# A linear-attention and gated long-convolution kernel: head pairs with packed tails, crossbar transposes, a maximum added by matmul, a DFT split by parity, and a planned order

## The chip, the cores and the metric

One core of one Trainium2 chip. The metric is the device time of one execution in microseconds (us), the median of several; executions fall into a fast and a slow state, and only fast ones are compared. Engines: PE (TensorE), DVE (VectorE), ACT (ScalarE), POOL (GpSimd), SP (SyncE, which here only issues transfers). DMA is the set of 16 transfer engines; the profile counts every queue's packets against them.

## The reference, cut to what matters

```python
# q, k, v: 8 batches x 8 heads x 576 x 64; w_phi 64 x 128
def phi(x):
    proj = einsum('bhsd,df->bhsf', x, w_phi)
    proj = proj - max(abs(proj), axis=-1, keepdims=True)
    return concatenate([exp(proj), exp(-proj)], axis=-1)
q_p, k_p = phi(q), phi(k)
kv = einsum('bhsf,bhsd->bhfd', k_p, v);  z = sum(k_p, axis=2)
attn = (q_p @ kv) / (q_p @ z + 1e-06)           # -> x: 8 x 576 x 512
x1, x2, x3 = split(x @ w_proj, 3)               # w_proj 512 x 1536
x2_conv = irfft(rfft(x2, axis=1) * rfft(filter_fft, axis=0), axis=1)
out = (x1 * x2_conv * x3) @ w_out               # w_out 512 x 512
```

Two halves: attention per batch and head, then a gating block per batch. The maximum over 128 features makes rows of q and k comparable; the convolution is done as a DFT by matmul.

## The kernel before

Heads go in pairs. For a pair, q and k are transposed on PE against an identity and evicted by ACT. The 576 rows are five chunks of 128 (the last half empty), each handled by instructions of its own. The code is shortened; lines are left out inside and between the functions.

```python
def load_stage(nc, pools, q, k, v, b):
    for (src, dst) in ((q, qs), (k, ks), (v, vs)):
        for (ci, s0, rows) in s_chunks():                 # 15 loads a batch, rows of 64
            nc.gpsimd.dma_start(out=dst[0:rows, ci, :, 0:HDIM],
                in_=src[b, :, s0:s0 + rows, :].rearrange("h p d -> p h d"))

def tr_group(nc, pools, cdict, stage_t, hp, zero_pad, name):
    for (ci, s0, rows) in s_chunks():
        nc.tensor.transpose(trp[:, ci, :], blk, ident)
    nc.scalar.copy(dst, trp.rearrange("p c x -> p (c x)"))

# pk_group: wpp is block-diagonal, so both heads of a pair use all 128 rows
        nc.tensor.matmul(dst, lhsT=kT[:, s0:s0 + PART], rhs=wpp, start=True, stop=True)
# pqn_group: the maximum of q only scales one of the two signs afterwards
    nc.scalar.activation(cq, mxq, AF.Exp, bias=0.0, scale=2.0)
# nem_group, nep_group: one pass a sign, joined on DVE
    nc.vector.tensor_tensor(out=tmp, in0=full_view, in1=cq_b, op=ALU.mult)
    nc.vector.tensor_tensor(out=NEt, in0=full_view, in1=tmp, op=ALU.add)
    nc.vector.tensor_tensor(out=out_view, in0=num_view, in1=r_b, op=ALU.mult)
# xt_group: the attention's result is transposed on PE as well
        nc.tensor.transpose(trp[:, ci, :], x_nat[:, ci, t * PART:(t + 1) * PART], ident)
# g_fwd: six groups of five matmuls a batch (3 cosine, 3 sine)
            for kt in range(5):
                nc.tensor.matmul(acc, lhsT=mat[:, kt, m * PART:(m + 1) * PART],
                                 rhs=x2n[:, kt, :], start=(kt == 0), stop=(kt == 4))
```

The gating block of batch b is interleaved with the attention of batch b+1. A round below is one such pair.

## Time and profile before

| | before |
|---|---|
| time, median of 3 (range) | 506.72 us (505.07 to 511.94) |
| busy PE / DVE / ACT / POOL | 402.8 / 357.6 / 307.3 / 200.3 us |
| transfers issued by POOL (q0) | 114432 packets, 47.4% of the DMA engines' time |
| head, until the first gating matmul | 73.4 us |
| seven rounds | 56.7 us each; 50.9 in the last two |
| tail, the last gating block alone | 35 us |

Busy is the union of an engine's instructions, matmul ends being modelled. A round that waits for nothing is the busiest engine's work plus its gaps; the head is a chain, where latencies add up. The lines that carry this are in the prediction.

### The profile page before, as it was taken

To read this page: it belongs to the slowest core of one execution; us is meant where nothing else is said; L and a number is where in the kernel's file an instruction comes from. 1 tells how busy PE (TensorE), PEld (TensorE's weight loads), DVE (VectorE), ACT (ScalarE), POOL (GpSimd) and SP (SyncE) were. 2 spreads that over 40 slices of the span, in tenths; PEclk is the share of its full clock that TensorE was granted. 3 is DMA by queue.
4 is the path that set the end of the run, shared out by engine and by line. 5 is a ranking of instruction groups with operands and counts; after the bars stand their busy time and mean duration, and the time that the engine had idled before them with its cause. 6 is when DMAs were issued, how large, how long until landed. Compare 5 with 4: busy or idle time off the path is not lost.

```text
span 505.9 us, 9253 instructions
## 1 busy us (share of the span) xinstructions
PE 402.8 (80%) x3672; PEld 240.8 (48%) x3734; DVE 357.6 (71%) x546; ACT 307.3 (61%) x611; POOL 200.3 (40%) x212
## 2 busy tenths in 40 slices
PE   1566559988688796879798795888888898889995
PEld 0344435555355553545455463554545554555442
DVE  2267654497567884697859785697777986798664
ACT  1669858877079633985189352994279636963220
POOL 9789921158012860346312760246512211221000
PEclk9856659999899998998999798998999999999999
DMA  9999970059610893039900796019910011001102
GB/s 84 176 144 95 95 47 1 0 33 78 75 54 1 53 94 89 2 21 75 124 19 1 50 75 113 1 11 74 99 53 2 2 43 53 0 2 43 53 1 95
DMA packets 119724, 26.92 MB, mean 53 GB/s; under 512 B 113472, under 2 KB 114560, under 8 KB 119680
## 3 DMA queue, kind: packets, MB, share of 16 engines
q0 software_dynamic: 114432, 16.88, 47.4%
q1 hardware_dynamic: 5248, 9.44, 5.4%
q8 instruction: 29, 0.48, 0.4%
q14 instruction: 15, 0.12, 0.1%
HBM read 33.75 MB, written 9.44 MB: 85 GB/s over the span
## 4 chain that ended last, share of the span: by engine, by line
PE 48%; DVE 20%; ACT 15%; DMA 6%; POOL 6%; issue 5%; DVEq 0%; POOLq 0%; ACTq 0%
PE acc L598 7%; PE acc L656 7%; PE acc L568 6%; DVE x_nat L404 5%; PE acc L613 5%; DMA out_dram<-o 4%; ACT Epk L274 3%; PE acc L689 3%; ACT Emk L276 3%; PE trp L256 3%; DVE mxk L278 2%; PE xtr L411 2%; PE acc L540 2%; PE KV L355 2%; DVE NEt L397 2%
## 5 line engine op out<-in xcount | busy, mean ns | idle before, releaser
L414 ACT COPY xT<-xtr 128x640 bf16<-128x640 bf16 x32 | 22.5, 702 | 78.6 <-PE xtr L411 78.6
L278 DVE TENSOR_REDUCE mxk<-Pk_m 128x8 f32<-128x1024 f32 x32 | 39.1, 1221 | 41.8 <-ACT Emk L276 41.7
L337 DVE TENSOR_REDUCE mxq<-Pqn_m 128x8 f32<-128x1024 f32 x32 | 39.0, 1218 | 14.7 <-PE Pqn_m L335 14.4
L411 PE MATMUL xtr<-ident,x_nat 128*128 128x128 bf16 x160 | 16.3, 240 | 39.9 <-DVE x_nat L404 39.9
L598 PE MATMUL acc<-wproj_sb,xT 128*128 128x512 bf16 x153 | 44.3, 411 | 3.6 <-ACT qT L258 3.3
L240 POOL DMA_DIRECT2D qs<-in_q_dram x40 | 34.5, 874 | 27.4 <-PE trp L256 20.1
L274 ACT ACTIVATE Epk<-Pk_m 128x1024 bf16<-128x1024 f32 x32 | 32.7, 1022 | 19.2 <-PE Pk_m L272 19.2
L689 PE MATMUL acc<-wout_sb,yT 128*128 128x512 bf16 x146 | 39.8, 388 | 3.4 <-DVE yT L661 2.5
L602 DVE CAST x2n<-acc 128x512 bf16<-128x512 f32 (+1 forms) x40 | 26.9, 687 | 20.2 <-PE acc L598 20.1
L694 DVE COPY o<-acc 128x512 f32<-128x512 f32 (+1 forms) x40 | 27.2, 679 | 18.9 <-DMA out_dram<-o 9.4
L240 POOL DMA_DIRECT2D ks<-in_k_dram x40 | 33.9, 878 | 10.1 <-PE trp L256 10.1
L404 DVE TENSOR_TENSOR x_nat<-NEt,r 128x640 bf16<-128x640 f32 x32 | 35.6, 1111 | 0.6
L319 ACT ACTIVATE Eq<-Pq_m 128x1024 bf16<-128x1024 f32 x32 | 34.1, 1065 | 2.9 <-PE Pq_m L313 2.9
L568 PE MATMUL acc<-xT,wproj_sb 128*128 128x512 bf16 x120 | 35.3, 421 | 0.4
L240 POOL DMA_DIRECT2D vs<-in_v_dram x40 | 34.1, 881 | 2.8 <-POOL v_518 L296 0.6
L321 ACT ACTIVATE Eqm<-Pq_m 128x1024 bf16<-128x1024 f32 x32 | 33.8, 1058 | 0.0
L411 PEld LDWEIGHTS <-x_nat 128*128 128x128 bf16 x160 | 10.9, 106 | 48.0 <-DVE x_nat L404 46.1
L540 PE MATMUL acc<-xT,wproj_sb 128*128 128x512 bf16 x121 | 31.4, 378 | 2.7 <-ACT x1s L544 2.4
L613 PE MATMUL acc<-x2n,fwdS 128*128 128x512 bf16 x117 | 29.1, 378 | 5.3 <-ACT Cxs L617 5.0
L276 ACT ACTIVATE Emk<-Pk_m 128x1024 bf16<-128x1024 f32 x32 | 33.1, 1033 | 0.0
L661 DVE TENSOR_TENSOR yT<-acc,ts 128x512 bf16<-128x512 f32 x32 | 22.0, 688 | 12.8 <-PE acc L656 7.8
L572 DVE TENSOR_TENSOR ts<-acc,x1s 128x512 bf16<-128x512 f32 x32 | 22.0, 690 | 12.1 <-PE acc L568 10.0
(315 smaller groups left out, 1066.0 us busy)
## 6 DMA issues: line engine op xcount, KB each, us to landing
out_dram<-o SPq DMA_DIRECT2D x32, 256.0 KB, 2.0
qs<-in_q_dram POOLq DMA_DIRECT2D x32, 128.0 KB, 4.1
ks<-in_k_dram POOLq DMA_DIRECT2D x32, 128.0 KB, 4.5
vs<-in_v_dram POOLq DMA_DIRECT2D x32, 128.0 KB, 4.8
wproj_sb<-in_moe_w_proj_dram POOLq DMA_DIRECT2D x4, 384.0 KB, 8.3
out_dram<-o SPq DMA_DIRECT2D x8, 128.0 KB, 2.2
qs<-in_q_dram POOLq DMA_DIRECT2D x8, 64.0 KB, 3.9
ks<-in_k_dram POOLq DMA_DIRECT2D x8, 64.0 KB, 4.2
```

The costliest lines, as they stand in the source:

```text
L240: nc.gpsimd.dma_start(out=dst[0:rows, ci, :, 0:HDIM], in_=src[b, :, s0:s0 + rows, :].rearrange("h p d -> p h d"))
L274: nc.scalar.activation(Epk[:, 0:4, :], Pk_m, AF.Exp, bias=0.0, scale=1.0)
L276: nc.scalar.activation(Emk[:, 0:4, :], Pk_m, AF.Exp, bias=0.0, scale=-1.0)
L278: nc.vector.tensor_reduce(out=mxk[:, 0:4, :], in_=Pk_m.rearrange("p c (h f) -> p c h f", h=2), axis=AX.X, op=ALU.max, apply_absolute_value ...
L337: nc.vector.tensor_reduce(out=mxq[:, 0:4, :], in_=Pqn_m.rearrange("p c (h f) -> p c h f", h=2), axis=AX.X, op=ALU.max, apply_absolute_valu ...
L404: nc.vector.tensor_tensor(out=out_view, in0=num_view, in1=r_b, op=ALU.mult)
L411: nc.tensor.transpose(trp[:, ci, :], x_nat[:, ci, t * PART:(t + 1) * PART], ident)
L540: nc.tensor.matmul(acc, lhsT=wproj[:, kt, m * PART:(m + 1) * PART], rhs=xT_sb[:, kt, 0:512], start=(kt == 0), stop=(kt == 3))
L568: nc.tensor.matmul(acc, lhsT=wproj[:, kt, 1024 + m * PART:1024 + (m + 1) * PART], rhs=xT_sb[:, kt, 0:512], start=(kt == 0), stop=(kt == 3))
L598: nc.tensor.matmul(acc, lhsT=xT_sb[:, kt, s0:s0 + PART], rhs=wproj[:, kt, 512:1024], start=(kt == 0), stop=(kt == 3))
L613: nc.tensor.matmul(acc, lhsT=mat[:, kt, m * PART:(m + 1) * PART], rhs=x2n[:, kt, :], start=(kt == 0), stop=(kt == 4))
L689: nc.tensor.matmul(acc, lhsT=yT[:, kt, s0:s0 + PART], rhs=wout[:, kt, :], start=(kt == 0), stop=(kt == 3))
```

## The change

The intent is to take work off PE and DVE: transposes of q, k and the attention's result go to the DMA crossbar; the two heads of a pair sit in the two 64-row halves of PE; the tails of 64 rows of different heads are packed; q's maximum is added inside PSUM by a matmul, so that both signs accumulate in one numerator; the DFT is split into even and odd frequencies over folded inputs (17 matmuls for 30); and one list, PLAN, fixes the order on every engine. The core of the diff, shortened, with lines left out inside the functions too:

```diff
-        for (ci, s0, rows) in s_chunks():
-            nc.gpsimd.dma_start(out=dst[0:rows, ci, :, 0:HDIM], ...)
+    def load(self, n, b):                       # one load of rows of 256 elements
+        main = src[:, 0:512, :].rearrange("h (p j) d -> p h (j d)", j=4)
+        self.nc.gpsimd.dma_start(out=self.at(n + "n", b)..., in_=main)
-        nc.tensor.transpose(trp[:, ci, :], blk, ident)
-    nc.scalar.copy(dst, trp.rearrange("p c x -> p (c x)"))
+    def tr(self, n, b, i=None):
+            self.nc.sync.dma_start_transpose(out=self.at(n + "T", b), in_=self.at(n + "n", b))
...
+    def nat(self, n, b, hp):
+        for w_ in range(2):
+            for jj in range(2):
+                for jp in range(2):
+                    a = (2 * w_ + jj) * 128
+                    r = slice(64 * jp, 64 * jp + 64)
+                    self.mm(self.pb(jp, a, a + 128), x[r, (2 * hp + w_) * 2 + jj, :], w[r, :],
+                            True, True)
+    def Pq(self, b, hp):                        # q transposed, minus its maximum
+        for jp in range(2):
+            self.mm(self.pb(jp), w[r, :], x[r, 4 * hp:4 * hp + 4, :], start=True, stop=False)
+        for w_ in range(2):
+            for jp in range(2):
+                self.mm(self.pb(jp, 256 * w_, 256 * w_ + 256), sel[r, 2 * hp + w_, :],
+                        mT[r, jp:jp + 3:2, :], start=False, stop=(w_ == 1))
-    nc.vector.tensor_tensor(out=NEt, in0=full_view, in1=tmp, op=ALU.add)
+    def NE(self, b, hp):                        # both signs in one PSUM group
+                for s, g in enumerate("pm"):
+                    self.mm(self.pb(w, 65 * j, 65 * j + 65), ..., KVs[:, hp, w, s, :],
+                            start=(s == 0), stop=(s == 1))
+    def trx(self, b, hp):
+        self.nc.sync.dma_start_transpose(out=self.at("xT", b)[:, hp, :]..., in_=self.at("xn", b)...)
+    def fold(self, b, odd):                     # even and odd parts, on POOL
+        self.nc.gpsimd.tensor_tensor(out=o, in0=x[:, :, :, 0:56], in1=x[:, :, :, 72:128], op=op)
...
+        for word in PLAN.split():
+            name, _, bank = word.partition("@")
+            getattr(self, f)(*[int(a) if a.isdigit() else a for a in args])
```

The start of PLAN (a word is an operation, a batch, a part and a PSUM bank):

```
load,k,0 gen_phase filt_load gen_rows zeros gen_half load,q,0 gen_cols@0 w_load,phi load,v,0
gen_cols_ev@0 gen_angles loadt,k,0 tr,k,0 loadt,v,0 loadt,q,0 tr,q,0 w_load,proj gen_sin Pk,0,1@2
... w_load,out ... load,v,1 load,k,1 ... load,q,1 ... Qn,0,0@4 ... mlo,0 trm,0 ... tr,k,1
```

## The prediction

> **What bounds the kernel now.** I read, in this order: the busy line and the slices of the page; the core split into head, steady stretch and tail; the waits and the chain; the timeline of the tensor engine, for the pace of each kind of matmul; last the DMA queues.
>
> ```profile
> PE 402.8 (80%) x3672; PEld 240.8 (48%) x3734; DVE 357.6 (71%) x546; ACT 307.3 (61%) x611; POOL 200.3 (40%) x212
> ...
> q0 software_dynamic: 114432, 16.88, 47.4%
> ```
>
> PE is the busiest engine and DVE is not far below; one queue, the POOL-issued loads, holds the DMA engines for half the span.
>
> ```profile
> 0.00:73.40 73.40, 37.62 (x290) 25.18 (x293) 38.74 (x80) 46.90 (x88) 59.04 (x81) 0.70 1.36 110
> 312.00:363.00 51.00, 45.52 (x434) 27.54 (x438) 39.17 (x56) 34.36 (x70) 23.67 (x23) 0.93 0.52 36
> 420.00:470.00 50.00, 44.45 (x444) 26.93 (x449) 40.94 (x59) 34.88 (x71) 11.54 (x8) 1.00 0.06 20
> 470.00:506.00 36.00, 29.29 (x184) 14.08 (x187) 19.44 (x28) 6.82 (x12) 0.00 (x0) 0.97 0.13 45
> ```
>
> Columns: window, length, busy us of PE, PEld, DVE, ACT, POOL, clock, DMA share, GB/s. The first gating-block matmul (L598) starts at 73.4 us; until then only batch 0's attention and the set-up run. Seven rounds follow, each batch b's gating block beside batch b+1's attention: 73.4 to 470.7, 397 us, 56.7 a round. The last gating block runs alone for 35 us. In the chain of waits the rounds are 56 to 60 us long while loads run (chain entries "DMA vs" 5.2 us, "DMA out_dram" 5.9 and 6.3 us) and 50.9 once they have ended (x2 starts at 369.3, 420.2, 470.7 us). There PE is busy 89% and DVE 82%: the steady round is PE-bound, with DVE close behind.
>
> ```profile
> 231.31 0.44 PE L256 MATMUL trp<-ident,ks 128*128 128x128 bf16 x5
> 231.59 1.89 PE L568 MATMUL acc<-xT,wproj_sb 128*128 128x512 bf16 x7
> 233.31 0.60 PE L272 MATMUL Pk_m<-wpp,kT 128*128 128x256 bf16 x4
> 233.75 0.27 PE L272 MATMUL Pk_t<-wpp,kT 128*128 128x256 bf16 x1
> ...
> 234.16 0.63 PE L584 MATMUL acct<-xT,wproj_sb 128*128 128x64 bf16 x16
> 234.63 0.32 PE L355 MATMUL KV<-v_2722,Epk 128*128 128x65 bf16 x5
> 234.79 0.32 PE L355 MATMUL KV<-v_2724,Emk 128*128 128x65 bf16 x5
> ```
>
> The mean ns of a group is latency; the pace is start to start. 5 transposes in 0.28 us are 56 ns each; 4 of 256 columns in 0.44 are 110; 16 of 64 columns in 0.47 are 29; 5 of 65 in 0.16 are 32; 512 columns take 215 (8 matmuls, one unrecorded, in 1.72). Per batch, now: 60 transposes 3.4 us; k and q projections 40x110 = 4.4; transposed q 8x215+8x54 = 2.2; KV, NEm, NEp 160x32 = 5.1; x1 and x3 32x215+32x29 = 7.8; x2 4.3; forward DFT 30x215 = 6.4; inverse 24x215+24x29 = 5.9; output 4.3. Sum 43.8, against a 50.9 us round: PE at 86% of its own pace.
>
> ```profile
> 327.94 0.95 DVE L624 TENSOR_TENSOR t_4195<-Cxs,HC 128x1536 bf16<-128x1536 bf16 x1
> 328.80 2.03 DVE L626 TENSOR_TENSOR t_4197<-Cxs,HS 128x1536 bf16<-128x1536 bf16 x1
> ```
>
> ```profile
> 328.56 1.46 POOL L292 TENSOR_TENSOR v_4161<-vs,em 128x650 bf16<-128x650 bf16 x1 [5.12 <-ACT em L285]
> 329.98 1.99 POOL L296 TENSOR_TENSOR v_4163<-vs,mxe 128x650 bf16<-128x650 bf16 x1
> ```
>
> These are the timelines of DVE and of POOL in one stretch. The same DVE product takes 0.95 us alone and 2.03 beside POOL; the POOL product takes 1.28 alone (most of its groups) and 1.99 beside DVE.
>
> **What the Trainium skill says.** (1) "TensorEngine Tiling (Array Packing)", Overview and Tiling Modes: with a contraction of at most 64 rows the array runs as two 64-row tiles, up to 2x, but changing the tiling mode drains the engine. Every matmul of the attention here is 128*128, so this trace shows neither. (2) "SBUF — State Buffer", Who interferes with whom: DVE (two SBUF inputs) and GpSimd hold a shared port pair as an exclusive lock. The trace agrees: DVE's 2.03 us end at 330.83, 0.8 us after POOL's product has ended at 330.02, and POOL's next one runs 1.1 us past that. (3) "DMA: Bandwidth & Descriptors", Specifications: 512 B is the smallest efficient piece. 113472 of 119724 packets here are under it. (4) "VectorE: DVE Perf Modes", The three transpose paths: a crossbar transpose of 128x128 takes 1309 ns, one on TensorE 390. No transposing DMA is in this trace; PE's cost 219 ns of latency, 56 of pace, plus an eviction of 0.7 us for five.
>
> **The change, part by part (per batch).**
> *PE.* The 60 transposes go (-3.4 us). Natural k and q projections become 72 matmuls of 64 rows by 128 columns, 72x55 = 4.0 us one after another, 2.0 if the two row halves run together. Transposed q with the q maximum added by matmul: 8x215 + 18x110 + 4x55 = 3.9, or 2.0. KV stays 80x32 = 2.6. The numerator needs one pass (the exponent already holds the maximum; both signs accumulate in PSUM): 64x32 + 8x56 = 2.5. x1, x3 7.8, x2 4.3 and output 4.3 stay. The parity split takes the forward DFT from 30 to 17 matmuls (3.7) and the inverse from 24+24 to 20+20 (4.9). Sum 30.1 + 4.0 = 34.1 paired, 38.0 not. About 15 groups use half the rows; entering and leaving each may drain the array. The exposed part of a matmul's latency is 219-56 = 0.16 us, so at most 30x0.16 = 4.8; I take 2. PE: 36 (40 unpaired) against 43.8.
> *ACT.* 12 transpose evictions go (12x0.7 = 8.4), and 16 tail exponentials of about 0.4 become 2 of 1024 columns. Left: 18 exponentials at 0.95 start to start = 17.1; 7 tiny ones 1.5; from the plan 107 of 152 evictions of 512 columns in eight batches, 13.4x0.63 = 8.4, and KV's 0.8. Sum 28, against 35 now.
> *DVE.* 8 maxima of 1024 at 1.15 = 9.2 and two of 512, 1.2; reciprocals 1.0; normalising straight out of PSUM 4x0.69 + 2x0.41 = 3.6; spectral products five, 4x0.68 + 0.42 = 3.1, plus about 3 of lock waits (POOL is in use some 60% of the time, one product 1 to 2 us); ts and yT products 6.3; evictions 45/8 x 0.66 + KV's and tails' 1.2 = 4.9. Sum 32, against 42. tmp, NEt (3.3 each) and half the spectral products are what goes.
> *POOL.* v scaling: 4x(1024/650x1.28 = 2.0) and two tails 2.7; folds 3.5+1.4; t2 products 4x1.0; three loads at 0.87, six small at 0.6. Sum 26: no bound.
> *DMA.* Main loads move 1 KB rows in place of 256 B: 24576+12288 packets in place of 114432. Crossbar transposes add 1.9 MB a batch through the SP queue in ten issues; an estimate from the skill's 1309 ns for 32 KB taken as latency, not pace, is that they fit. They put 2 to 4 us of latency after each head pair, which the order hides in the steady state and not in the head.
>
> **The sum.** Steady round: 36 us of PE at 88%, the share it now reaches in the undisturbed windows (the planned order and fewer packets should keep it there all through, not only at the end) = 41. Seven rounds: 287. Head: the plan issues the first gating matmul after batch 0's attention; ACT needs by then about 31 us (18+4 exponentials, sines, filter evictions), DVE 29 after the first k projection. k lands at about 7 us (q's first megabyte takes from 1.3 to 10.4 now, in four times the packets), its transpose at about 13, a guess; then q maxima, the maximum's transpose, exponentials, normalising and the last transposes chain to 48-50. I take 52 (now 73.4). Tail: PE 7.8+4.3+3.7+4.9+4.3 = 25, plus fold, last eviction and store about 7 = 32 (now 35). 52+287+32 = 371; I add 3 for queue accidents: 374.
>
> **Rivals.** (a) The halves don't run together and mode changes drain fully: PE 38+5 = 43, /0.88 = 49 a round, 52+343+32 = 427. Against it: the code alternates row halves and banks on purpose. (b) DVE or its lock with POOL becomes the bound: POOL grows from 20 to 26 us a batch, so 32 may become 38 with waits; at 88% that is 43: 388. (c) Crossbar transposes are slow or queue behind stores on SP: the round grows by waits on xT, and the head by two 512 KB transposes; 8 us of head and 3 a round give 403. For it: nothing in this trace measures them. (d) Everything fits: PE 34 at 92% = 37, head 46: 46+259+31 = 336. (e) No gain, because loads bound the rounds: against it, the 50.9 us rounds without loads were PE's.
>
> **Range and chances.** All of (a) to (c) still leave it more than 2% below 506.7, so faster has 0.96; the rest is for a plan that stalls on the chip. 8 in 10: 340 to 415, from mostly (d) to a half of (a) with (c).
>
> **What would show it.** After: PE busy below 330 us and above 80% of the steady windows; 64*128 projections in pairs a few ns apart (paired) or 54 apart (not); ACT near 28, DVE near 32 a batch; no wait of PE on xT over 3 us; first gating matmul near 52 us. Wrong would be: PE idle with DVE or ACT over 90% busy, long waits for the transposing DMA, or a mean clock below 0.9.

## The result, and the profile after

The changed kernel takes 418.28 us (416.79 to 419.22, 4 runs) against 507.88 (505.07 to 511.94, 4 runs) on the same chip: ratio 0.8259, 95% interval 0.8197 to 0.8321. A ratio here is the mean time of one kernel's fast runs over that of the other's of the same rounds, so not quite the ratio of the medians. The direction was right; the time lies 44 us above the predicted 374 and 3 us outside the range.

The page of the kernel after, busy time and queues:

```profile
PE 323.1 (77%) x3367; PEld 176.0 (42%) x3367; DVE 270.1 (65%) x426; ACT 222.5 (53%) x340; POOL 226.7 (54%) x237
...
q0 software_dynamic: 39232, 16.29, 33.9%
q1 hardware_dynamic: 72328, 27.08, 32.9%
```

PE lost 80 us, DVE 88, ACT 85. The packets that POOL issues fell to a third, but q1, which had 5248 packets before, now carries 72328: those are the crossbar transposes, with the filter's loads and the stores of the result. The two queues together take 67% of the DMA engines' time where 53% was taken before.

The same windows as in the prediction: head, a round with loads, a late round, tail (columns: window, length, busy us of PE, PEld, DVE, ACT, POOL, clock, DMA share, GB/s; overlapping packets can bring the DMA share above 1):

```profile
0.00:86.60 86.60, 28.86 (x342) 21.66 (x343) 40.04 (x91) 34.36 (x50) 44.14 (x59) 0.89 1.13 153
...
133.00:179.00 46.00, 39.73 (x427) 20.89 (x427) 32.69 (x49) 25.86 (x38) 26.10 (x26) 0.95 0.67 100
...
348.00:387.40 39.40, 38.33 (x406) 20.11 (x405) 29.04 (x43) 26.05 (x42) 21.02 (x19) 1.00 0.24 52
387.40:417.20 29.80, 25.31 (x162) 11.98 (x159) 11.46 (x17) 11.48 (x20) 10.20 (x9) 0.98 0.24 80
```

Head 86.6 us (predicted 52), seven rounds 300.8, 43.0 each (predicted 41), tail 29.8 (predicted 32). The differences are 34.6, 14 and -2; less the reserve of 3 that the prediction had added, they make the 43 us by which the span misses 374. The head is even longer than before. Rounds with loads take 44 to 47 us, the late ones without loads 38 to 40, the last with PE at 97%. Of the signs that the prediction named, PE below 330 us held (323.1); the first gating matmul near 52 us did not, PE waits for xT up to 4.8 us where 3 was the limit, and long waits for the transposing DMA, named as a sign of being wrong, are there (24.1 us for k's, below).

The head after, on PE's timeline (start, length, what, in brackets the idle time before it and what ended it), and on SP's, where the length is how long the queue's issue was held:

```profile
35.49 1.89 PE L522 MATMUL ps<-wphi,kT 64*128 64x128 bf16 x32 [24.11 <-DMA kT<-kn]
44.85 0.61 PE L522 MATMUL ps<-wphi,qT 64*128 64x128 bf16 x8 [7.47 <-DMA qT<-qn]
...
84.67 1.04 PE L522 MATMUL ps<-wphi,qT 64*128 64x128 bf16 x16 [9.92 <-DMA qT<-qn]
86.60 1.86 PE L791 MATMUL ps<-xT,wproj 128*128 128x512 bf16 x4 [0.89 <-DVE mq L595]
```

```profile
10.60 7.28 SPq L407 DMA_DIRECT2D fl<-in_moe_filter_fft_dram  x8
17.99 9.32 SPq L505 DMA_TRANSPOSE kT<-kn  x1
27.41 8.15 SPq L505 DMA_TRANSPOSE qT<-qn  x1
...
70.60 5.59 SPq L505 DMA_TRANSPOSE qT<-qn  x1
```

The first k projection starts at 35.5 us. Its transpose is issued at 18.0, behind 26 small loads of the filter, and lands 17.5 us later; q's comes after it. Over all eight batches k's 512 KB transpose holds SP for a median of 1.9 us, and in a late round one of q's is seen to land in 4.3. The third PE line belongs to batch 1: in PE's fixed order its q projection stands ahead of the first gating matmul, and waits 9.9 us for its own transpose.

### The profile page after: what moved, and what is told of

The parts are those of the page before. It is cut to its first block, busy times and chain, and to the rows that moved or that the text cites. A ratio compares the mean times of both kernels' runs of the same rounds, so it can differ in the third digit from the quotient of the medians.

```text
span 417.2 us, 8401 instructions
## 1 busy us (share of the span) xinstructions
PE 323.1 (77%) x3367; PEld 176.0 (42%) x3367; DVE 270.1 (65%) x426; ACT 222.5 (53%) x340; POOL 226.7 (54%) x237
## 3 DMA queue, kind: packets, MB, share of 16 engines
q1 hardware_dynamic: 72328, 27.08, 32.9%
## 5 line engine op out<-in xcount | busy, mean ns | idle before, releaser
L791 PE MATMUL ps<-xT,wproj 128*128 128x512 bf16 x256 | 66.5, 393 | 10.7 <-DMA xT<-xn 8.2
L595 DVE TENSOR_REDUCE mq<-ps 128x8 f32<-128x1024 f32 x32 | 38.5, 1219 | 31.8 <-PE ps L522 27.0
L582 DVE TENSOR_REDUCE mk<-ps 128x8 f32<-128x1024 f32 x32 | 38.6, 1216 | 26.0 <-PE ps L522 20.6
L755 PE MATMUL ps<-wproj,eo 128*128 128x512 bf16 (+1 forms) x160 | 41.9, 405 | 6.0 <-POOL eo L739 5.9
L779 POOL TENSOR_TENSOR t<-C,B 128x512 bf16<-128x512 bf16 x32 | 38.8, 1228 | 13.5 <-ACT C L671 11.3
L570 ACT ACTIVATE Eqm<-ps 128x1024 bf16<-128x1024 f32 x32 | 32.5, 1031 | 17.1 <-PE ps L553 17.1
L837 PE MATMUL ps<-inv,Y 128*128 128x512 bf16 x160 | 39.5, 388 | 1.6 <-DVE Y L785 1.6
L858 PE MATMUL ps<-wout,yT 128*128 128x512 bf16 x160 | 38.9, 386 | 0.0
L522 PE MATMUL ps<-wphi,qT 64*128 64x128 bf16 x256 | 14.5, 245 | 25.7 <-DMA qT<-qn 21.0
L434 PE MATMUL ps<-x2n,fwd 128*128 128x512 bf16 (+1 forms) x136 | 34.1, 380 | 0.0
L522 PE MATMUL ps<-wphi,kT 64*128 64x128 bf16 x256 | 13.3, 235 | 26.2 <-DMA kT<-kn 24.1
L570 ACT ACTIVATE Eqp<-ps 128x1024 bf16<-128x1024 f32 x32 | 32.5, 1033 | 1.0 <-PE ps L553 1.0
```

The lines of the kernel that those rows point to most:

```text
L434: self.mm(self.pb(0), l, r, start=(i == 0), stop=(i == len(ks) - 1))
L570: self.nc.scalar.activation(self.at("E" + n + g, i).rearrange("p a b c f -> p a (b c f)"), self.db(), AF.Exp, bias=0.0, scale=1.0 if g == ...
L582: self.nc.vector.tensor_reduce(out=o, in_=self.db().rearrange("p a (w j f) -> p a w j f", w=2, j=2), axis=AX.X, op=ALU.max, apply_absolute ...
L595: self.nc.vector.tensor_reduce(out=o, in_=self.db().rearrange("p a (w j f) -> p a w j f", w=2, j=2), axis=AX.X, op=ALU.max, apply_absolute ...
L755: self.mm(self.pb(0, p1=n), eo[:, kt, a:a + n], w[:, kt, 512:1024], start=(kt == 0), stop=(kt == 3))
L779: self.nc.gpsimd.tensor_tensor(out=self.at("t2", b)[:, t, :], in0=self.at("C", b)[:, t ^ 1, :], in1=self.at("B")[:, t, :], op=ALU.mult)
```

## The experiments

Fifteen kernels ran, each on the same chip as runs of the kernel before. Unless said otherwise an edit starts from the changed kernel, the result is correct, and the profiled run is fast. "Head" is the start of the first gating matmul, "rounds" the time from there to the first gating matmul of the last block; the tail after that is 29.5 to 30.5 us in every run and is left out.

| run | head | rounds | median us | ratio to before (95%) |
|---|---|---|---|---|
| the changed kernel | 86.6 | 300.7 | 418.28 | 0.8259 (0.8197 to 0.8321) |
| e1 filter loads on ACT's queue | 89.8 | 302.8 | 422.06 | 0.8333 (0.8265 to 0.8401) |
| e2 loads late | 76.7 | 306.6 | 414.23 | 0.8183 (0.8107 to 0.8258) |
| e3 both | 80.8 | 309.5 | 416.02 | 0.8229 (0.8162 to 0.8296) |
| e4 no loads after batch 1 (wrong) | 77.4 | 275.4 | 384.44 | 0.7593 (0.7544 to 0.7642) |
| e5 order on SP | 85.9 | 299.2 | 414.23 | 0.8147 (0.8082 to 0.8212) |
| e6 loads after the folds | 77.1 | 313.1 | 424.15 | 0.8343 (0.8278 to 0.8408) |
| e7 e2 + e5 + e6 | 74.6 | 305.2 | 411.67 | 0.8111 (0.8035 to 0.8187) |
| e8 halves one after the other | 86.1 | 298.7 | 418.19 | 0.8224 (0.8162 to 0.8286) |
| e9 one half only (wrong) | 84.3 | 319.6 | 435.64 | 0.8539 (0.8482 to 0.8595) |
| e10 no q, k transposes after batch 1 (wrong) | 85.6 | 274.6 | 391.97 | 0.7689 (0.7638 to 0.7741) |
| e11 e7 without later loads (wrong) | 76.4 | 272.6 | 378.54 | 0.7428 (0.7371 to 0.7485) |
| e12 e11 without later transposes (wrong) | 74.8 | 265.4 | 372.14 | 0.7312 (0.7251 to 0.7373) |
| e13 filter late | 87.3 | 306.7 | 424.68 | 0.8357 (0.8308 to 0.8407) |
| e14 e7 without later transposes (wrong) | 76.3 | 279.1 | 386.91 | 0.7605 (0.7554 to 0.7656) |
| e15 filter behind the maxima | 83.3 | 306.0 | 425.33 | 0.8350 (0.8305 to 0.8396) |

One run each of e3, e5 and e7 was slow (422.08, 421.3 and 419.11 us) and is left out of the median. e3's profile is of its slow run, so its head and rounds are not compared with the others.

### What holds the head: e1, e2, e3

```diff
 e1, e3: filt_load
-        sp, f, s = self.nc.sync, self.dram["filt"], self.scr
+        sp, f, s = self.nc.scalar, self.dram["filt"], self.scr
 e2, e3: PLAN
-... tr,q,0 w_load,proj ... w_load,out ... load,v,1 load,k,1 ... load,q,1 loadt,q,1 ... vs,p,0,0
+... tr,q,0 ... vs,p,0,0 w_load,proj load,k,1 load,v,1 load,q,1 loadt,q,1 w_load,out
```

> The 26 filter loads leave the SP queue for the ACT queue; nothing else moves. Theory SP order (the first k transpose waits 18.0 us only because 26 filter issues stand before it): k's transpose issues at about 10 us, the first k projection moves from 35.5 to about 27, and the total falls by about 8 us, to 410. Theory shared DMA engines (the engines are over 95% busy from 5 to 50 us, so an earlier issue only waits longer): the first k projection stays within 3 us of 35.5 and the total within 3 us of 418.

> The loads of batch 1's q, k, v and of both weights go behind the first scaled values on POOL, so that they do not run beside the first transposes. Theory shared DMA engines: k's transpose still issues at 18 but lands in 5 to 7 us in place of 17.5, the first k projection is at about 24, the first q projection at about 30 in place of 44.9, and the first gating matmul falls from 86.6 to about 76; total about 408. Theory SP order: the transposes keep their 17 us, the first k projection stays near 35, the total near 418 or above it, because the moved loads come later.

> Both edits. If SP order and shared engines each cost on their own: first k projection near 16, first gating matmul near 68, total near 400. If only one of them matters, the total equals the better of the two single edits within 3 us.

In e1 the k transpose is issued at 9.1 us instead of 18.0 and k is projected at 20.7 instead of 35.5, yet the head ends 3 us later. That is no verdict on the order, for the edit did move something else. The issues of the loads now hold ACT itself, until 39.0 us; its first exponential of k starts at 43.8 us (36.6 in the changed kernel), and q's first projection waits on PE for these exponentials. The longest hold on ACT, and that wait:

```profile
2.96 18.01 ACTq L407 DMA_DIRECT2D fl<-in_moe_filter_fft_dram  x8
```

```profile
47.89 0.61 PE L522 MATMUL ps<-wphi,qT 64*128 64x128 bf16 x8 [25.34 <-ACT Ekp L570]
```

q's transpose took 25.7 us to land, but it landed at 37.7, 10 us before q was projected. e3 holds ACT in the same way until 26.9 us.

In e2, which leaves SP alone, k lands in 4.5 us instead of 17.5 and is projected at 21.7. So the slow landing was the other loads in flight, not the transpose; and 14 us saved at k became 9.9 at the end of the head, of which the rounds took 5.9 back. The head came as the theory of shared engines had it (76.7 for 76), the total did not (414.23 for 408). e3 gains nothing over e2 (416.02 for 414.23, the intervals of the ratios overlap). No run put k's projection before 18.8 us, whatever the order.

### What holds the rounds: e4

```diff
 PLAN: the 36 words load,{q,k,v},b and loadt,{q,k,v},b with b from 2 to 7
-... load,k,2 ... load,q,2 ... load,v,2 ... load,v,7 ...
+(left out: the later batches read the old tiles; wrong on purpose)
```

> Wrong result on purpose: the loads of batches 2 to 7 are left out, the transposes read the old data, so all work but the loads stays. Theory that loads beside transposes stretch the rounds: the seven rounds fall from 43.0 to about 39 us each (what the last two, with few loads, take: 38.0 and 39.4), and the head loses the loads of batch 2 and 3 (first gating matmul from 86.6 to about 78); total about 381. Theory that PE alone sets the round: rounds stay at 43 within 1 us, total above 405.

384.44, near the 381 of the theory that loads stretch the rounds. Its rounds take 275.4 us in place of 300.7, 3.6 less each.

### Order inside the head: e5, e6, e7

```diff
 e5, e7 (SP): the result of batch 0 before q of batch 1; POOL not held by the load of q of batch 3
-... trx,0,1 ... tr,q,1 trx,0,0 ... trt,q,1 trx,0,2 ... load,q,3 ... trxt,0 Qn,1,0@2 ... fold,0,1
+... trx,0,1 trx,0,0 ... trx,0,2 ... trxt,0 tr,q,1 trt,q,1 Qn,1,0@2 ... fold,0,1 ... foldt,0,0 load,q,3
 e6, e7: load,q,2 load,v,2 their tails, loadt,k,2, load,k,3, load,q,3 behind foldt,0,0
```

> Edit: the transposes of q of batch 1 are put behind all transposes of xn of batch 0 on SyncE, and the load of q of batch 3 (which held GpSimd until q of batch 1 was transposed, 12.7 us) behind the folds of batch 0. Same bytes, same work. Theory 'order': the head is long because urgent transposes stand behind less urgent ones and behind a held GpSimd; then the first fold moves from 87.5 to about 77 us and the time falls to 407-411. Rival 'capacity': the DMA engines are full until 87 us whatever the order; then the first fold stays at 85-88 and the time at 415-420.

> Edit: the loads of q and v of batch 2, of the tails of batch 2 and of k and q of batch 3 are issued after the folds of batch 0 instead of before them. Theory 'loads crowd the transposes': q of batch 1 lands about 5 us after its issue instead of 14, the first fold moves from 87.5 to about 78 us, and the time falls to 408-413. Rival 'the bytes have to move anyway': what the head gains the first round gives back, 415-420.

> Edit: the loads of batch 1 and of the two gate weights after k of batch 0 (as in e2, 414.2), the order on SyncE of e5 and the later loads of e6 together. Theory 'order and crowding': first fold at about 66-70 us, time 396-402. Rival 'capacity': no lower than e2, 412-416.

The expectations of a lasting gain fell (they count to the first fold, POOL's sum over xT of batch 0, which stands at 87.5 us in the changed kernel and at 82.0, 80.5 and 68.2 here). By the first gating matmul e5 wins 0.7 us, e6 9.5 and e7 12.0; the rounds then take back nothing in e5, 12.4 in e6 and 4.5 in e7. POOL is 19.3 us earlier in e7, but PE has batch 1's q projection ahead of the gating block and uses only 12.0 of it. e7 is still the fastest correct version: 411.67 us, 1.8% by the ratios (0.8111 for 0.8259, from different rounds) below the changed kernel.

### Are the halves run together: e8, e9

```diff
 e8: nat, natt, Pq, Pqt
-        for w_ in range(2):
-            for jj in range(2):
-                for jp in range(2):
+        for jp in range(2):
+            for w_ in range(2):
+                for jj in range(2):
 e9: the same four functions (wrong on purpose)
-                    r = slice(64 * jp, 64 * jp + 64)
+                    r = slice(0, 64)
```

> Edit: the matmuls of 64 rows are issued all of the lower half first, then all of the upper half, so that no two neighbours use different halves; same work, same results. Theory 'neighbouring halves run side by side': TensorE busy rises by about 3.9 us a round (the saving worked out in the prediction) and by 31 us in all, from 323 to about 354; as the early rounds wait for transfers, part of it hides: time 430-446. Rival 'they do not overlap, the records only look so' or 'TensorE bounds nothing': busy about 323-330 or time 416-422.

> WRONG on purpose: every 64-row matmul reads weights and data of the lower half (rows 0 to 63), so that no two can run side by side in different halves; same count, same columns. e8 showed that the order in which the halves are issued does not matter, so it was no test of the pairing. Theory 'halves run side by side whatever their order': TensorE busy rises by about 3.9 us a round, 31 us in all, to about 354, and the time to 432-446. Rival 'no overlap at all': 416-422 and busy 320-326.

PE's timeline in the changed kernel, in e8 and in e9: blocks of two matmuls of 512 columns and four of 256, and the start of what comes next:

```profile
101.74 0.38 PE L549 MATMUL ps<-qT,wphi 64*128 64x512 bf16 x2
101.95 0.38 PE L553 MATMUL ps<-mT,sel 64*128 64x256 bf16 x4
102.17 0.38 PE L549 MATMUL ps<-qT,wphi 64*128 64x512 bf16 x2
102.39 0.38 PE L553 MATMUL ps<-mT,sel 64*128 64x256 bf16 x4
102.70 1.90 PE L791 MATMUL ps<-xT,wproj 128*128 128x512 bf16 x8
```

```profile
152.23 0.39 PE L549 MATMUL ps<-qT,wphi 64*128 64x512 bf16 x2
152.45 0.39 PE L551 MATMUL ps<-mT,sel 64*128 64x256 bf16 x4
152.66 0.39 PE L549 MATMUL ps<-qT,wphi 64*128 64x512 bf16 x2
```

```profile
247.56 0.59 PE L549 MATMUL ps<-qT,wphi 64*128 64x512 bf16 x2
247.99 0.60 PE L553 MATMUL ps<-mT,sel 64*128 64x256 bf16 x4
248.42 0.59 PE L549 MATMUL ps<-qT,wphi 64*128 64x512 bf16 x2
248.85 0.60 PE L553 MATMUL ps<-mT,sel 64*128 64x256 bf16 x4
249.38 0.83 PE L434 MATMUL ps<-x2n,fwd 128*128 128x512 bf16 x3
```

A block that another such block follows takes 0.43 us from start to start, 0.43 in e8 and 0.86 with one half. At 215 ns for 512 columns, 0.43 us is the time of the 1024 columns of one half, so the two halves run wholly side by side, and in e9 one after the other. (The first block after a wait can take 0.60, in the changed kernel at 287.23 and in e8 at 284.41.) e8 was no test of the pairing: its program gives one half's 512 columns and its two of 256 before the other half's first, but the trace starts both 512s ahead of all 256s, in the same time. So the halves are served side by side whatever their order in the program, in a block this short. e9 is the test: without a second half PE is busy 350.1 us instead of 323.1 (27 more, with 45 matmul records missing from its trace; 31 had been expected) and the time rises by 17.4 us (14 by the ratios). The pairing is real, and 10 to 13 of its 27 us lie beside other waits.

### Loads against transposes: e10, e11, e12, e14

```diff
 e10, PLAN (24 words; from the changed kernel)
-... tr,k,2 ... trt,q,2 ... trt,k,2 ... tr,q,2 ... tr,k,7 ... trt,k,7 trt,q,7 ... tr,q,7
 e11, PLAN: from e7, the 36 words of e4
-... load,k,2 ... load,q,2 ... load,v,7 ...
 e12: e11 and e10 together; e14: from e7, the 24 words of e10
```

> WRONG on purpose: the crossbar transposes of q and k (mains and tails) are left out for batches 2 to 7, which use the old ones; all loads stay. Theory 'the DMA engines are shared and their work costs time': per batch 4400 packets of some 34 ns over 16 engines, about 9.5 us of all engines, fall away in six rounds, half as much as e4 removed, so about half of e4's gain: 398-406. Rival 'only the slow loads crowd': 414-420. Rival 'the landing of q and k is itself the path': 380-390.

> WRONG on purpose: e4 (loads of batches 2 to 7 left out) with the order of e7 in the head. Theory 'shared DMA': first fold at 64-68 us as in e7, rounds of 39 as in e4, time 366-374, so the prediction's 374 is what the kernel would take with free transfers. Rival 'head order only moves waiting from the head to the rounds': 381-386 as e4.

> WRONG on purpose: e11 with the transposes of e10 left out as well. If rounds of 39 are TensorE's own (38.3 busy a round), nothing is left to gain: 360-370. If q's and k's transposes still cost waits in e11: 345-358.

> WRONG on purpose: e7 without the transposes of q and k for batches 2 to 7, which completes the square of e7 (loads and transposes, 412.9), e11 (no loads, 378.5) and e12 (neither, 372.1). If the two costs were independent, leaving out the transposes would give the 6.4 us that it gave between e11 and e12: 406. If they hurt by colliding on the shared engines, it gives most of e11's gain as well: 378-392.

e7, e11, e12 and e14 share the head's order and form a square:

| | transposes of q, k | none after batch 1 |
|---|---|---|
| loads | 411.67 (e7) | 386.91 (e14) |
| no loads after batch 1 | 378.54 (e11) | 372.14 (e12) |

Taking away the loads gives 33.1 us, taking away the transposes 24.8; both together 39.5, not 57.9. With the loads gone the transposes cost only 6.4; with the transposes gone the loads cost 14.8. So 18.4 us of the 39.5 are there only when both are: not two independent costs. Only e14 fell in a range of its expectation, that of a collision; e10 (391.97) gained more than the theory of shared engines said, e11 (378.54) and e12 (372.14) gained less than theirs.

That the two collide on the DMA engines is likely, but the square alone does not show it, since the program also ties them. The load of a new q waits on POOL for the transpose that still reads its buffer, and this exists only when both are there: in e7 three such waits of 30.0 us in all between 90 and 345 us, and a fourth of 8.1 us whose end the trace puts down to nothing; in e11, e12 and e14 none. And on SP some transposes of q stand ahead of the result's. The traces speak for the engines. After three of the four, POOL still waits 6.0, 6.9 and 5.5 us for transposes of the result before it can fold, so these three did not delay the folds. And the result's transposes, issued between 87 and 345 us, land in a median of 4.9 us in e7 and in 2.7, 2.4 and 2.4 in e14, e11 and e12, as far as the traces show landings. No run breaks the ties with both kinds of transfer kept. The slices of the DMA engines' busy share (tenths, 40 slices), e7 and e12:

```profile
DMA  9967999996995497853973857723833143103403
```

```profile
DMA  8974999400043102421140034002230131105103
```

With both kinds of transfer the engines are mostly full until after the middle; with neither, only in the head. e12's windows of 85 to 215 and 215 to 345 us, which hold almost all of its seven rounds:

```profile
85.00:215.00 130.00, 124.47 (x1442) 68.74 (x1461) 103.63 (x158) 90.05 (x138) 71.82 (x64) 1.00 0.20 48
215.00:345.00 130.00, 125.55 (x1345) 67.77 (x1364) 101.60 (x156) 83.24 (x128) 65.56 (x60) 1.00 0.24 60
```

PE is busy 250 of 260 us at full clock (its trace, too, lacks 45 of 3367 matmul records): with the transfers out of the way, PE bounds the rounds. They take 265.4 us, 37.9 each, against 43.0 in the changed kernel: the transfers cost 5.1 us a round. What can't be told apart is the share of the granted clock in this. Its mean is 0.942 in the changed kernel and 0.975 in e12, and it is low where PE has just waited: 0.5 in the two slices from 73 to 94 us of the changed kernel; PE stands still in the first of them.

### The filter's loads: e13, e15

```diff
 e13, from e7
-load,k,0 gen_phase filt_load gen_rows ... filt_fold ... trt,q,0 ... H,3@0 ... H_fix ... Pk,1,1@0
+load,k,0 gen_phase gen_rows ... trt,q,0 filt_load ... vs,m,0,0 filt_fold ... H,3@0 ... H_fix Pk,1,1@0
 e15, from e13
-... trt,q,0 filt_load ... trm,0 ...
+... trt,q,0 ... trm,0 filt_load ...
```

> Edit on top of e7, results kept right: the 26 loads of the filter stand behind the transposes of k, q and their tails of batch 0 on SyncE, their folds behind all scaling of v of batch 0, and the filter's DFT behind the exponentials of q of batch 0. Theory 'the start of the head is a queue too': k is transposed by about 13 us in place of 21.6, q by 16, and the first fold starts at about 58-62 us instead of 68; by the capacity theory most of it is given back in the first rounds: 406-412. If the head's gain stays: 400-405. Rival 'k and q are bound by ScalarE and VectorE in the head': first fold stays at 66-70, time 410-416.

> Edit on top of e13, results kept right: the filter's loads now stand behind the transpose of q's maxima of batch 0 too, which in e13 waited on SyncE from 36.5 to 47.6 us for them. Theory 'a queue served in order': the maxima land by about 42 us in place of 56.9, the first fold starts at 60-66 us (e13 81.3, e7 68.2), and the time is 402-412 (below e7's 412.9 if the first rounds don't take it back). Rival 'it is the sharing alone, the bytes of filter and gate weights must pass before the fold': first fold at 68 or later, time 412-418.

Neither came out as the theory of a queue had it: 424.68 and 425.33 lie above every range. k's transpose is issued at 7.2 us instead of 17.1, but k is projected at 19.2 and 18.8, only some 2.5 us earlier than in e7 (21.6). q's maxima are ready 4.6 us sooner in e13 (38.3 instead of e7's 42.9; the 36.5 of the expectation is when the first half of them is), and wait 9.3 us on SP for the filter's loads; e15 mends that and PE has them at 46.0 instead of e7's 50.8. Then, in e15, the transposes of the result are held:

```profile
52.44 5.43 SPq L401 DMA_DIRECT2D fl<-in_moe_filter_fft_dram  x8
57.98 3.19 SPq L499 DMA_TRANSPOSE kT<-kn  x1
61.26 14.24 SPq L716 DMA_TRANSPOSE xT<-xn  x4
```

Four small transposes hold SP for 14.2 us, where e7 needs 6.7. The filter's 26 loads have to pass somewhere in the head, and ahead of everything is the least bad of the places tried.

### What is left of the head when nothing crowds it

PE in e11, waits only:

```profile
21.07 1.89 PE L514 MATMUL ps<-wphi,kT 64*128 64x128 bf16 x32 [9.69 <-DMA kT<-kn]
31.75 0.61 PE L514 MATMUL ps<-wphi,qT 64*128 64x128 bf16 x8 [8.79 <-ACT Ekp L562]
...
51.56 0.40 PE L557 MATMUL ps<-mT,sel 64*128 64x128 bf16 x4 [7.26 <-DMA mT<-mh]
...
74.45 1.04 PE L514 MATMUL ps<-wphi,qT 64*128 64x128 bf16 x16 [6.61 <-DMA qT<-qn]
76.38 1.86 PE L783 MATMUL ps<-xT,wproj 128*128 128x512 bf16 x4 [0.89 <-DVE mq L587]
```

Even so the first gating matmul is at 76.4, not 52: k 21 us in, q held 8.8 us by ACT's exponentials of k, which free the PSUM banks (5.0 of them ACT itself waits for DVE's maxima of k), the maxima's transpose 7.3, and at the end again batch 1's q ahead of the gating block. e12 gives 74.8.

## Why the prediction was wrong, point by point

- **Head, "I take 52": this step failed, and it is the larger part of the miss (34.6 us).** The prediction had k transposed "at about 13, a guess" and the chain behind it to 48-50. k was there at 35.5. k itself lay ready at about 7 us, as predicted (e13 issues its transpose at 7.2); the transpose then stood behind the filter's loads on SP until 18.0 and took 17.5 us to land. 12 us of the 34.6 are order and crowding (86.6 against 74.6 in e7); the other 22.6 remain in the best head found: k at 21 in place of 13, 8.8 us of ACT before q, a transpose of the maxima that keeps PE waiting 7.3 us where 2 to 4 of latency were taken, and 6.6 us for a q of the next batch, which the sum left out. These waits are read from e11's trace; no run takes them away one by one.
- **DMA, "they fit": failed.** Latency was taken for the whole cost. The square shows that the transposes of q and k and the loads cost time, and more when both are there: 33.1 and 24.8 us when removed alone, 39.5 together. By the queues' shares, the loads of one batch are 16.6 us of all engines' packet time ((0.339 x 417.2 - 0.109 x 382.4) / 6, from the changed kernel and e4), q's and k's transposes 7.3 ((0.329 x 417.2 - 0.240 x 389.8) / 6, with e10). Rival (c) named this and gave it 8 us of head and 3 a round; its round of 44 is near the measured 43.0, its head of 60 is not.
- **Round, 41 us: measured 43.0, by two errors that partly cancel.** PE's work was right: 36 predicted, 36.4 in e12 (250 / 260 x 37.9). Its share without crowding was too low, 96% for 88%, which makes rounds of 37.9 (7 x 3.1 = 22 us less in all); the transfers then add 7 x 5.1 = 36, among which a busy time of 38.4 a round at lower clock. The difference is the 14.
- **Pairing: right.** Predicted 3.9 us of PE a round; e9 shows 27 us in all, 3.4 for each of eight batches. The change between full and half rows costs about what was allowed. After the eight full-row matmuls from 102.70, at 215 ns each, the next half-row block starts 0.11 us late (104.53); and a block takes 0.53 us when full rows follow, 0.43 when half rows do. The changed kernel's rounds have 11 such groups each, which makes an estimate of 2.3 us for the 2 taken.
- **DVE, ACT, POOL: right.** Over the rounds 31.2, 25.2 and 24.6 us each (218.6, 176.7 and 172.3 over 7) for 32, 28 and 26. Rival (b) did not occur.
- **Tail: 30 for 32**, right.
- **Rivals (a) and (d).** e9 rules out (a). (d), everything fits, had rounds of 37, which e12 shows to be the kernel's own; e12's 372.1, so near the predicted 374, is no confirmation, since its head is 23 us longer and its rounds 22 us shorter than the prediction's.

Still open: how much of the 18.4 us is what the two kinds of transfer share, the engines themselves or the memory behind them, and how much is the program's ties between them; and how much of the 5.1 us a round is the lower clock rather than waiting.

## What to carry to other kernels

Moving transposes from an engine to the DMA crossbar is not free work: add up the packet time of everything that shares the DMA engines, per stage, and ask what else is in flight when an urgent transpose is issued. In a head, order moves waits about more than it removes them; compare where the steady state ends, not only where it starts (12.0 us won there in e7 left 7.5). An experiment that reorders independent instructions need not show anything about their overlap, as in e8: make them compete for the same rows instead. And an edit that moves transfers to another engine's queue also holds that engine's own work, as in e1: look at that engine before reading the result.

## What the Trainium skill lacked or had wrong

- "TensorE: Matmul & The Clock Gate", The mechanism, says that matmuls start and end strictly in program order. In e8 the second half's 512-column matmul, fourth in the program's block, starts before the second, and the block takes the same 0.43 us as with alternating halves (0.86 when all use one half). No run tells how far this reaches beyond six instructions, nor whether the tool chain had changed the order before the chip saw it.
- "DMA: Bandwidth & Descriptors", Issuing engines are not separate DMA queues, says that issuing from several engines saves only the time of the issue, which it calls usually small. Here it was not small: in e1 the issues of eight filter loads held ACT for 18.0 us (SP for 5.6 and 7.3 in the changed kernel).
- That page has no figure for a crossbar transpose beside loads. Here a 512 KB transpose lands in 4.3 us with little in flight and in 17.5 in the crowded head, and holds SP's issue for 1.7 to 9.3 us. The prediction's 1309 ns was for one tile of 128x128; 16 such tiles in 4.3 us are about 0.27 us each.
- Neither that page nor the tiling page of the prediction gives a cost for the change of tiling mode; about 0.1 us each way here.
